# The last block's second layer gives x transposed, and the chain to the experts stands in program order

## The chip, the cores and the metric

The kernel runs on one core of one Trainium2 chip. The metric is device time in microseconds (us) of one execution, all inputs and outputs in device memory. TensorE (PE) does the matrix products, VectorE (DVE), ScalarE (ACT) and GpSimd (POOL) work elementwise, SyncE (SP) issues the transfers. Each engine works its own list of instructions in order; semaphores tie the lists together.

## The reference

Three stages in a row, all fp32: windowed attention with block summaries, a feed-forward layer with the activation h·cos(h), and a soft mixture of experts.

```python
# attention: 4 batches x 8 heads, 768 positions, 64 wide
k_sum = k.reshape(B, H, nb, 32, D).max(axis=3);  v_sum = v.reshape(B, H, nb, 32, D).mean(axis=3)
a = softmax(concat(local scores (|i-j| < 16), scores against k_sum + log 32))
x = a @ concat(v, v_sum)                       # -> 3072 tokens x 512

h = x @ w_in                                   # 512 -> 2048
x = (h * np.cos(h)) @ w_out                    # 2048 -> 512

logits = x @ phi                               # 8 experts x 4 slots = 32 columns
d = softmax(logits, over the 3072 tokens);  slot_input = d.T @ x          # 32 x 512
slot_out[e] = np.maximum(slot_input[e] @ w1[e], 0) @ w2[e]                # 512 -> 1024 -> 512
c = softmax(logits, over the 32 slots);     out = c @ slot_out            # 3072 x 512
```

## The kernel before

The 3072 tokens are worked in 6 blocks of 512 (`NB`), the hidden width in 16 pieces of 128 (`NF`), which makes 96 slots. In slot s the first layer (`mm1`, L378) makes a piece h of 128 hidden rows by 512 tokens from 12 matmuls, the elementwise engines turn it into g = h·cos(h) (`act1` and `act2`), and the second layer (`mm2`, L416) of slot s - 2 adds 12 matmuls into the four accumulators `acc`, one for each 128 tokens. Twelve, because each fp32 operand is split into two numbers of the reduced-width type fp32r, a high and a low part: gh is a copy of g (ACT), gl is g - gh (GpSimd), and the weights are split in the same way (`split_w`: wih, wil for the first layer, woh, wol for the second). Three products of parts make one fp32 product.

In `mm2` the tokens of gh or gl are the stationary operand and the weights move, so `acc[t]` holds 128 tokens as rows and the 512 features as columns. At the end of a block `x2_out` copies the four accumulators to x2. The mixture's part for a block (`m2_*`, L450 to L519) then makes: x2T, x turned around by 16 PE transposes (xt) and four copies; the logits, 32 slots by 512 tokens, stored as 128 rows of (token tile, slot) by 128 tokens; the running maximum over tokens m and its negation nm; e = exp(logits - m) with its sum z; the combine weights c (softmax over the slots, from the transposed logits ltt), kept in `call` until the end; d, e transposed; and `sacc`, the running sum of d·x, corrected by al = exp(old m - new m).

For the blocks 0 to 4 these steps are spread over the slots of the next block by a table of half-slots (`at`, `at2`, `sched_m2`). For block 5 they stand behind the loop (L732 to L786). There the maxima of the four token tiles are joined (pst, mxr, mrow, wg, wsel), the sum is normalized (psl, rz) and the 32 slot inputs slT come out. The experts follow: `hp` (L809) multiplies slT by w1, `yp` (L842) by w2, both with the expert weights `ex` as the moving operand, and the output projection (`op`, L866) multiplies the transposed combine weights cT by the split slot outputs.

cT comes from `cT_mm` and `cT_split`: for each block 16 small matmuls `ct` (32 columns of c against the identity, written four times below each other), one ACT copy that rounds to fp32r, and two DVE subtractions that leave the low parts in two of the four groups of rows. The 64 expert tiles of 512 KB each are loaded by `grab` into whatever buffer comes free; the last 36 of these loads are issued behind 690 us.

The order: the program is built by a scheduler with a timeline simulation, which places each engine's instructions. From slot 17 (`MAN0`) to the end of the loop the orders of PE and SP are those of the program text instead. Everything before slot 17, and the tail behind the loop, is the scheduler's, with a few `issue_after` hints (L736 to L786). The start is a list of short words (`PRE`); `magic` (L104, L106) is a constant that no instruction reads, since `NACT` is 0.

Of the kernel before, what the change touches and what calls it, by code (L numbers as in the profile page):

```python
# [44 lines left out]
NACT = 0  # L45
NABS = 0
# [32 lines left out]
def body(ctx: ExitStack, tc: tile.TileContext, q0, qk, kT, vn, vx, w, phi, ex, cst, out):  # L79
# [311 lines left out]
    def act1(s):  # L391
        h = hps[s]
        a = ring.tile([128, TB], F32, name=f"a{s}", tag="a")
        if s < NACT:
            nc.scalar.activation(a, h, AF.Identity, bias=magic)
            nc.vector.scalar_tensor_tensor(out=a, in0=a, scalar=MAGIC, in1=h, op0=ALU.subtract, op1=ALU.subtract)
            if s < NABS:
                nc.scalar.activation(a, a, AF.Abs)
            else:
                nc.vector.tensor_single_scalar(out=a.bitcast(I32), in_=a.bitcast(I32), scalar=0x7FFFFFFF, op=ALU.bitwise_and)  # L400
        else:
            nc.vector.tensor_scalar(out=a, in0=h, scalar1=0.25, scalar2=MAGIC, op0=ALU.add, op1=ALU.add)  # L402
            nc.vector.scalar_tensor_tensor(out=a, in0=a, scalar=MAGIC, in1=h, op0=ALU.subtract, op1=ALU.subtract)  # L403
        nc.scalar.activation(a, a, AF.Sin, bias=halfpi, scale=-TWO_PI)  # L404
        gs[s] = a

    def act2(s):
# [4 lines left out]
        nc.scalar.copy(gh, a)  # L412
        nc.gpsimd.tensor_tensor(out=gl, in0=a, in1=gh, op=ALU.subtract)  # L413
        gs[s] = (gh, gl)

    def mm2(s):  # L416
# [24 lines left out]
    call = m2.tile([128, 4 * NB, 32], F32, name="call", tag="call")  # L441
# [14 lines left out]
    def m2_logits(j):  # L456
        ps = ps_m.tile([128, 512], F32, name="lt", tag="m")
        lt = ps[:, 0:128]
        for k in range(4):
            for t in range(4):  # L460
                product = nc.tensor.matmul(ps[32 * t:32 * t + 32, 0:128], phis[:, k, :], x2T[:, t, k, :],
                                           start=k == 0, stop=k == 3)
        lts = stat.tile([128, 128], F32, name="lts", tag="lts", bufs=1)
        nc.scalar.copy(lts, lt)
        m = stat.tile([128, 1], F32, name=f"m{j}", tag="m")
        nc.vector.reduce_max(out=m, in_=lt, axis=AX.X)
        if j:
            nc.vector.tensor_tensor(out=m, in0=m, in1=run["m"], op=ALU.max)
        nm = stat.tile([128, 1], F32, name=f"nm{j}", tag="nm")
        nc.vector.tensor_scalar_mul(nm, m, -1.0)  # L470
        run.update(mold=run.get("m"), m=m, nm=nm, lts=lts)
        return product

    def m2_lT(j):
        ps = ps_m.tile([128, 512], F32, name="ltt", tag="m")
        nc.tensor.transpose(ps[:, 0:128], run["lts"], ident)
        c = call[:, 4 * j:4 * j + 4, :]
# [5 lines left out]
    def m2_exp(j):  # L483
# [3 lines left out]
        nc.scalar.activation(e, lts, AF.Exp, bias=nm, accum_out=z)  # L487
        if j:
            al = stat.tile([128, 1], F32, name=f"al{j}", tag="al")
            nc.scalar.activation(al, run["mold"], AF.Exp, bias=nm)  # L490
            nc.vector.scalar_tensor_tensor(out=z, in0=run["z"], scalar=al, in1=z, op0=ALU.mult, op1=ALU.add)
            run["al"] = al
        c = call[:, 4 * j:4 * j + 4, :]
        nc.scalar.activation(c, c, AF.Exp)
        run.update(z=z, e=e)

    def m2_c(j):
        ps = ps_m.tile([128, 512], F32, name="dt", tag="m")
        nc.tensor.transpose(ps[:, 0:128], run["e"], ident)
        d = stat.tile([128, 128], F32, name="d", tag="d", bufs=1)  # L500
        nc.vector.tensor_copy(d, ps[:, 0:128])
        c = call[:, 4 * j:4 * j + 4, :]
# [4 lines left out]
        run["d"] = d  # L507
        nc.vector.tensor_tensor(out=c, in0=c, in1=cs.unsqueeze(2).to_broadcast([128, 4, 32]), op=ALU.mult)

    def m2_S(j):  # L510
        ps = ps_m.tile([128, 512], F32, name="sp", tag="m")
        for t in range(4):
            product = nc.tensor.matmul(ps[32 * t:32 * t + 32, :], run["d"][:, 32 * t:32 * t + 32], x2[:, t, :],
                                       start=True, stop=True)
        if j:
# [3 lines left out]
        return product  # L519
# [160 lines left out]
    for s in range(NSLOT + LAG):  # L680
# [12 lines left out]
        if s < NSLOT:  # L693
            act2(s)
# [249 lines left out]
```

## Time and profile before

| what | value |
|---|---|
| time, median of 3 runs | 781.09 us (780.65 to 781.32) |
| span of the profiled execution | 778.9 us |
| PE busy | 740.2 us (95%), 5517 instructions |
| DVE busy | 473.6 us (61%), 686 instructions |
| ACT busy | 433.4 us (56%), 786 instructions |
| POOL busy | 428.6 us (55%), 302 instructions |
| read from memory | 92.54 MB, written 6.29 MB, 127 GB/s over the span |

The profiled execution has no time of its own in the runs; its span on the engines, 778.9 us, is what its times are measured in, and it lies 2.2 us below the median of the runs.

A busy share of 95% is an average over stages. It is read beside the idle gaps of PE, of which the rows below show four large ones, beside the clock that PE was granted in each stretch, and, at the end, beside the question which PE work the next step waits for. In the rows "[1.36 <-ACT aT L342]" behind an instruction says that its engine had been idle for 1.36 us before it, and that the ACT step of line 342 ended this.

### The profile page before, as it was taken

What the parts mean: (1) busy time and instruction counts of PE and PEld (TensorE: products, weight loads), DVE (VectorE), ACT (ScalarE), POOL (GpSimd) and SP (SyncE); (2) the same over time, 40 slices, a digit from 0 to 9 for tenths busy, and PEclk for the clock granted to TensorE, in tenths of its full rate; (3) what the DMA queues carried; (4) which work ended last, traced back from release to release, by engine and by line L of the source; (5) the groups of instructions that cost most, each with busy time, mean ns of one, the idle gap of its engine ahead of it and who ended that gap; (6) DMA issues with size and microseconds to landing.
All of it is one profiled execution on the core that took longest, in us unless ns stands there. A gap on an engine that the chain in (4) does not pass through costs nothing.

```text
span 778.9 us, 13853 instructions
## 1 busy us (share of the span) xinstructions
PE 740.2 (95%) x5517; PEld 573.5 (74%) x5517; DVE 473.6 (61%) x686; ACT 433.4 (56%) x786; POOL 428.6 (55%) x302
## 2 busy tenths in 40 slices
PE   9977799998999999998999999999999999999994
PEld 7866678776877787776787777778768888786453
DVE  4578896767477576576575684774773444433523
ACT  4979868636465455574465555464554455443222
POOL 2555884365557657556566566665576665752000
PEclk9997999999999999999999999999999999999998
DMA  9988753121120331311211211301101922328978
GB/s 331 396 264 331 271 164 113 42 97 59 48 95 1 100 105 29 121 68 41 87 44 33 72 40 33 111 0 35 33 1 56 392 93 82 109 81 299 371 306 268
DMA packets 35585, 101.69 MB, mean 131 GB/s; under 512 B 3393, under 2 KB 13889, under 8 KB 33473
## 3 DMA queue, kind: packets, MB, share of 16 engines
q1 hardware_dynamic: 35520, 100.81, 36.8%
q8 instruction: 43, 0.70, 0.4%
q14 instruction: 22, 0.17, 0.1%
HBM read 92.54 MB, written 6.29 MB: 127 GB/s over the span
## 4 chain that ended last, share of the span: by engine, by line
PE 63%; DVE 13%; ACT 12%; DMA 6%; issue 4%; SPq 0%; ACTq 0%; DVEq 0%
PE acc L425 8%; PE h L384 8%; PE acc L426 8%; PE h L385 8%; PE acc L429 7%; PE h L388 7%; PE av L354 3%; DVE S L329 2%; DMA qk<-in_qk_dram 2%; PE yp L842 2%; DMA kr<-in_kT_dram 2%; PE sc L286 2%; PE hp L809 2%; ACT a L404 2%; DVE a L403 2%
## 5 line engine op out<-in xcount | busy, mean ns | idle before, releaser
L373 POOL TENSOR_TENSOR wol<-w,woh 128x512 fp32r<-128x512 f32 x96 | 143.9, 1500 | 115.0 <-ACT woh L372 115.0
L413 POOL TENSOR_TENSOR gl<-a,gh 128x512 fp32r<-128x512 f32 x96 | 129.0, 1343 | 83.8 <-ACT gh L412 78.3
L384 PE MATMUL h<-xh,wih 128*128 128x512 f32 x384 | 156.4, 407 | 6.7 <-DVE a L409 6.6
L425 PE MATMUL acc<-woh,gh 128*128 128x512 f32 x384 | 157.4, 410 | 3.5 <-DVE x L448 3.5
L385 PE MATMUL h<-xl,wih 128*128 128x512 f32 x384 | 152.2, 396 | 0.0
L426 PE MATMUL acc<-wol,gh 128*128 128x512 f32 x384 | 152.1, 397 | 0.0
L373 POOL TENSOR_TENSOR wil<-w,wih 128x512 fp32r<-128x512 f32 x81 | 113.9, 1406 | 42.8 <-PE h L388 24.2
L402 DVE TENSOR_SCALAR a<-h 128x512 f32<-128x512 f32 x96 | 65.9, 686 | 115.8 <-PE h L388 110.7
L404 ACT ACTIVATE a<-a,halfpi 128x512 f32<-128x512 f32 x96 | 69.4, 724 | 115.7 <-DVE a L403 115.4
L388 PE MATMUL h<-xh,wil 128*128 128x512 f32 x384 | 104.9, 395 | 0.0
L429 PE MATMUL acc<-woh,gl 128*128 128x512 f32 x384 | 104.6, 393 | 0.0
L409 DVE TENSOR_TENSOR a<-h,a 128x512 f32<-128x512 f32 x96 | 66.1, 689 | 57.0 <-ACT a L404 56.9
L425 PEld LDWEIGHTS acc<-woh,gh 128*128 128x128 f32 x384 | 72.4, 188 | 28.6 <-issue 11.8
L384 PEld LDWEIGHTS h<-xh,wih 128*128 128x128 f32 x384 | 72.7, 189 | 24.6 <-DVE a L409 8.4
L372 ACT CAST wih<-w 128x512 fp32r<-128x512 f32 x96 | 59.2, 617 | 47.2 <-PE h L385 46.4
L388 PEld LDWEIGHTS h<-xh,wil 128*128 128x128 f32 x384 | 72.5, 189 | 16.3 <-issue 0.2
L429 PEld LDWEIGHTS acc<-woh,gl 128*128 128x128 f32 x384 | 72.1, 189 | 16.4 <-issue 0.6
L385 PEld LDWEIGHTS h<-xl,wih 128*128 128x128 f32 x384 | 72.8, 190 | 15.2 <-issue 0.3
L426 PEld LDWEIGHTS acc<-wol,gh 128*128 128x128 f32 x384 | 72.6, 189 | 14.6 <-issue 0.6
L412 ACT CAST gh<-a 128x512 fp32r<-128x512 f32 x96 | 59.3, 619 | 32.8 <-DVE a L409 32.8
L372 ACT CAST woh<-w 128x512 fp32r<-128x512 f32 x96 | 59.1, 616 | 21.7 <-PE acc L429 20.8
L403 DVE SCALAR_TENSOR_TENSOR a<-a,h 128x512 f32<-128x512 f32 x96 | 65.5, 683 | 2.1
(137 smaller groups left out, 945.8 us busy)
## 6 DMA issues: line engine op xcount, KB each, us to landing
ex<-in_ex_dram SPq DMA_DIRECT2D x64, 512.0 KB
raw<-in_w_dram SPq DMA_DIRECT2D x16, 1024.0 KB
qk<-in_qk_dram SPq DMA_DIRECT2D x20, 736.0 KB
v<-in_vx_dram SPq DMA_DIRECT2D x24, 512.0 KB
kr<-in_kT_dram SPq DMA_DIRECT2D x16, 384.0 KB
vb<-in_vn_dram SPq DMA_DIRECT2D x12, 512.0 KB
out_dram<-o SPq DMA_DIRECT2D x12, 512.0 KB
v<-vs SPq DMA_DIRECT2D x40, 48.0 KB
```

What stands on the lines that cost most here:

```text
L372: nc.scalar.copy(hi, W[f][:, part, :])
L373: (eng or nc.gpsimd).tensor_tensor(out=lo, in0=W[f][:, part, :], in1=hi, op=ALU.subtract)
L384: nc.tensor.matmul(h, hi[:, c], xh[s // NF][:, t, :], start=t == 0, stop=False)
L385: nc.tensor.matmul(h, hi[:, c], xl[s // NF][:, t, :], start=False, stop=False)
L388: nc.tensor.matmul(h, lo[:, c], xh[s // NF][:, t, :], start=False, stop=t == 3)
L403: nc.vector.scalar_tensor_tensor(out=a, in0=a, scalar=MAGIC, in1=h, op0=ALU.subtract, op1=ALU.subtract)
L404: nc.scalar.activation(a, a, AF.Sin, bias=halfpi, scale=-TWO_PI)
L409: nc.vector.tensor_tensor(out=a, in0=h, in1=a, op=ALU.mult)
L413: nc.gpsimd.tensor_tensor(out=gl, in0=a, in1=gh, op=ALU.subtract)
L425: nc.tensor.matmul(acc[t], gh[:, c], hi, start=f == 0, stop=False)
L426: nc.tensor.matmul(acc[t], gh[:, c], lo, start=False, stop=False)
L429: nc.tensor.matmul(acc[t], gl[:, c], hi, start=False, stop=f == NF - 1)
```

## The change

- **Second layer of block 5.** `mm2` swaps the operands in the slots of the last block: the weights stand, gh and gl move. `acc[k]` then holds 128 features as rows and 512 tokens as columns, which is x transposed. In the last slot the three kinds of product are issued output by output, so that `acc[0]` is complete first.
- **Tail.** The four accumulators are copied straight to x2T (two on DVE, two on ACT), and the 16 transposes that made x2T are gone from block 5. x2, which the dispatch product needs, is made by transposing x2T back (`x2_back`, tiles xb) between the steps of the maximum. The `issue_after` hints are gone; from the table load of the exponential to the first cT copies, PE, DVE and ACT follow the program text.
- **Negated maximum.** `nm` comes negated from the reduction, and the running maximum is a running minimum of `nm`; the separate negation is gone in every block. The `m2_exp` and `m2_c` steps are cut into smaller functions.
- **Combine weights.** c is computed in a small tile `cw`, and `call` holds it already split: four columns groups (high, low, high, low), by one DVE cast and one GpSimd subtraction per block. `cT_mm` is then 4 transposes of 128x128 per block in place of 16 small matmuls, and `cT_out` one copy (DVE or ACT) in place of one ACT copy and two DVE subtractions.
- **Place of the combine weights.** The sets of blocks 0 to 2 stand around psl ahead of the experts; that of block 3, and block 5's own transposition, exponential and normalization, stand behind the first group of hp matmuls, the sets of blocks 4 and 5 two groups later.
- **Setup.** `magic` with its memset, `NACT` and `NABS` are gone; a size of descriptor memory (`dynamic_dma_scratch_size=512`) is set.

```diff
-    magic = const.tile([128, 1], F32, name="magic")
     nc.vector.memset(halfpi, math.pi / 2)
-    nc.vector.memset(magic, MAGIC)
@@ mm2
+        if s >= NSLOT - NF:
+            for k in range(4):
+                c = slice(128 * k, 128 * k + 128)
+                nc.tensor.matmul(acc[k], hi[:, c], gh, start=f == 0, stop=False)
+                nc.tensor.matmul(acc[k], lo[:, c], gh, start=False, stop=False)
+                if f == NF - 1:
+                    nc.tensor.matmul(acc[k], hi[:, c], gl, start=False, stop=True)
+            for k in range(4 if f < NF - 1 else 0):
+                nc.tensor.matmul(acc[k], hi[:, 128 * k:128 * k + 128], gl, start=False, stop=False)
+            return
@@
-    call = m2.tile([128, 4 * NB, 32], F32, name="call", tag="call")
+    call = m2.tile([128, 4 * NB, 4, 32], F32R, name="call", tag="call")
@@ m2_logits
+                nc.tensor.matmul(ps[32 * t:32 * t + 32, 0:128], phis[:, k, :],
+                                 x2T[:, k, t, :] if j == NB - 1 else x2T[:, t, k, :], start=k == 0, stop=k == 3)
...
+        nc.vector.tensor_reduce(out=nm, in_=lt, axis=AX.X, op=ALU.max, negate=True)
+        if j:
+            nc.vector.tensor_tensor(out=nm, in0=nm, in1=run["nm"], op=ALU.min)
         nc.scalar.copy(lts, lt)
@@ m2_norm
+        c2 = c.unsqueeze(2).to_broadcast([128, 4, 2, 32])
+        o = call[:, 4 * j:4 * j + 4].rearrange("p t (a b) s -> p t a b s", b=2)
+        nc.vector.tensor_copy(o[:, :, :, 0], c2)
+        nc.gpsimd.tensor_tensor(out=o[:, :, :, 1], in0=c2, in1=o[:, :, :, 0], op=ALU.subtract)
@@ m2_S
+        if j == NB - 1:
+            for c in (slice(0, 256), slice(256, 512)):
+                nc.vector.scalar_tensor_tensor(out=sacc[:, c], in0=sacc[:, c], scalar=run["al"], in1=ps[:, c],
+                                               op0=ALU.mult, op1=ALU.add)
@@ cT_mm, cT_out
         for t in range(4):
-            for r in range(0, 128, 32):
-                nc.tensor.matmul(ps[r:r + 32, 128 * t:128 * t + 128], call[:, 4 * j + t, :], ident, start=True, stop=True)
+            nc.tensor.transpose(ps[:, 128 * t:128 * t + 128],
+                                call[:, 4 * j + t].rearrange("p r s -> p (r s)").bitcast(F32), ident)
...
-        nc.scalar.copy(o, ps)
-        for r in (slice(32, 64), slice(96, 128)):
-            nc.vector.tensor_tensor(out=o[r, :], in0=ps[r, :], in1=o[r, :], op=ALU.subtract)
+        (nc.scalar.copy if j % 2 else nc.vector.tensor_copy)(o, cps.pop(j))
@@ the tail
+    chain = tc.manual_schedule(engines={EE.PE, EE.DVE, EE.Activation})
+    chain.__enter__()
+    with tc.issue_after(last_gh.ins):
+        nc.scalar.activation(warm, halfpi, AF.Exp)
+    nc.vector.tensor_scalar_mul(x2Tk[:, 0], acc[0], scale)
+    nc.scalar.mul(x2Tk[:, 1], acc[1], scale)
+    nc.vector.tensor_scalar_mul(x2Tk[:, 2], acc[2], scale)
+    nc.scalar.mul(x2Tk[:, 3], acc[3], scale)
+    m2_logits(NB - 1)
+    m2_e(NB - 1)
+
+    def x2_back(t):
+        ps = ps_acc.tile([128, 512], F32, name=f"xb{t}", tag=f"acc{t}")
+        for k in range(4):
+            nc.tensor.transpose(ps[:, 128 * k:128 * k + 128], x2T[:, k, t, :], ident)
+        (nc.scalar.copy if t % 2 else nc.vector.tensor_copy)(x2[:, t, :], ps)
+
+    x2_back(0)
+    m2_al(NB - 1)
+    x2_back(1)
...
+    m2_d(NB - 1)
+    x2_back(2)
...
+    x2_back(3)
...
+    m2_S(NB - 1)
+    cT_mm(0)
...
+    cT_mm(1)
+    cT_mm(2)
...
+    for j in range(3):
+        cT_out(j)
+    chain.__exit__(None, None, None)
@@ the experts, behind the first group of hp
-                for j in range(2, NB):
-                    cT_split(j)
+                cT_mm(3)
+                cT_out(3)
+                m2_lT(NB - 1)
+                m2_cexp(NB - 1)
+                m2_norm(NB - 1)
+            if g == 0 and k == 2:
+                for j in range(4, NB):
+                    cT_mm(j)
+                    cT_out(j)
```

The built order shows where the instructions came to stand. First PE at the end of the loop and in the tail. Names are out<-in; the numbers behind tile names only tell buffers apart. Before:

```order
L721 MATMUL ct_7013<-ident,call 32x128 x3
L721 MATMUL ct_7030<-ident,call 32x128
L429 MATMUL acc_0_6183<-woh_6844,gl_6827 128x512
L429 MATMUL acc_1_6184<-woh_6844,gl_6827 128x512
L429 MATMUL acc_2_6185<-woh_6844,gl_6827 128x512
L429 MATMUL acc_3_6186<-woh_6844,gl_6827 128x512
L721 MATMUL ct_7030<-ident,call 32x128 x15
L453 MATMUL xt<-ident,x_1882 128x128 x16
L461 MATMUL lt<-x2T,phis 32x128 x16
L721 MATMUL ct_7053<-ident,call 32x128 x16
L476 MATMUL ltt<-ident,lts 128x128
L746 MATMUL pst<-ident,m_6950 1x128
```

The same place now:

```order
L418 MATMUL acc_3_6188<-gl_6830,woh_6847 128x512
L460 MATMUL lt<-x2T,phis 32x128 x16
L769 MATMUL xb_6938<-ident,x2T 128x128 x4
L769 MATMUL xb_6947<-ident,x2T 128x128 x4
L776 MATMUL pst<-ident,nm_6931 1x128
L506 MATMUL dt<-ident,e 128x128
L769 MATMUL xb_6963<-ident,x2T 128x128 x4
L769 MATMUL xb_6971<-ident,x2T 128x128 x4
L788 MATMUL pst_6980<-ones,mrow 128x1
L530 MATMUL sp<-x_1880,d 32x512 x4
L742 MATMUL ct_6997<-ident,call 128x128 x4
```

The logits (lt) stand directly behind the last accumulating matmul, the ct matmuls of the combine weights are gone from the place ahead of them, and the transposes xb stand around the transpositions of the maximum (pst) and of e (dt).

The second place is not in the diff: the scheduler's order of ACT around 60 us, in the first slots of block 0. Here qk are the copies of key sums for the next pair of attention groups, S the exponentials of the pair before, w and cv steps of a weight conversion, and a the sine of the first slots. Before:

```order
L372 CAST wih_785<-w_583 128x512
L129 ACTIVATE w_879<-raw_749 128x1024
L130 ACTIVATE cv_880<-raw_749 128x1024
L372 CAST wih_845<-w_593 128x512
L319 ACTIVATE S_696,sm_797<-S_696,mx_717 128x120 x6
L234 COPY qk_569<-ks_269 128x4x24
L234 COPY qk_569<-ks_271 128x4x24
L319 ACTIVATE S_696,sm_797<-S_696,mx_717 128x120 x2
L404 ACT_TABLE_LOAD
L404 ACTIVATE a_692<-a_692,halfpi 128x512
```

And now:

```order
L368 CAST wih_783<-w_581 128x512
L230 COPY qk_567<-ks_267 128x4x24
L230 COPY qk_567<-ks_269 128x4x24
L368 CAST wih_843<-w_591 128x512
L315 ACTIVATE S_694,sm_795<-S_694,mx_715 128x120 x8
L125 ACTIVATE w_877<-raw_747 128x1024
L126 ACTIVATE cv_878<-raw_747 128x1024
L392 ACT_TABLE_LOAD
L392 ACTIVATE a_690<-a_690,halfpi 128x512
```

The two qk copies moved ahead of all eight exponentials and of the conversion of the third weight (w, cv), which in turn moved behind the exponentials.

The third place is PE in the slot at 83 us, where the second layer begins. Here vs_1 are sums of the values of the next batch, and av the attention output. Before:

```order
L388 MATMUL h_1000<-xh_464,wil_931 128x512
L184 MATMUL vs_1_942<-vb_1_915,avg 32x128 x8
L388 MATMUL h_1000<-xh_464,wil_931 128x512 x3
L425 MATMUL acc_0_892<-woh_934,gh_888 128x512
L425 MATMUL acc_1_893<-woh_934,gh_888 128x512
L354 MATMUL av_977<-aT_0_866,v_665 64x64
```

And now:

```order
L384 MATMUL h_998<-xh_462,wil_929 128x512 x4
L424 MATMUL acc_0_890<-woh_932,gh_886 128x512
L425 MATMUL acc_0_890<-wol_933,gh_886 128x512
L424 MATMUL acc_1_891<-woh_932,gh_886 128x512
L425 MATMUL acc_1_891<-wol_933,gh_886 128x512
L424 MATMUL acc_2_892<-woh_932,gh_886 128x512
L425 MATMUL acc_2_892<-wol_933,gh_886 128x512
L424 MATMUL acc_3_893<-woh_932,gh_886 128x512
L425 MATMUL acc_3_893<-wol_933,gh_886 128x512
L428 MATMUL acc_0_890<-woh_932,gl_887 128x512
L428 MATMUL acc_1_891<-woh_932,gl_887 128x512
L180 MATMUL vs_1_940<-vb_1_913,avg 32x128 x8
```

The eight matmuls with gh now stand together ahead of the attention's, instead of two of them and then av; the value sums came behind them.

## Rows read from the trace of the kernel before

**Rows 1.** The view by stretch: stretch, length, busy us of each engine, clock, DMA.

```profile
core 0: us, PE busy (x) PEld busy (x) DVE busy (x) ACT busy (x) POOL busy (x), PEclk, DMA share, GB/s
60.00:69.00 9.00, 6.64 (x43) 5.30 (x44) 8.54 (x12) 8.97 (x19) 3.06 (x3) 0.50 0.97 369
83.00:89.50 6.50, 2.20 (x38) 1.59 (x38) 5.34 (x7) 5.95 (x9) 6.50 (x4) 1.00 0.94 334
89.50:93.00 3.50, 3.50 (x11) 2.82 (x10) 3.46 (x4) 2.80 (x5) 3.50 (x3) 0.51 0.89 356
660.00:700.00 40.00, 40.00 (x179) 31.66 (x178) 15.96 (x24) 18.19 (x30) 25.55 (x21) 1.00 0.28 93
717.00:720.00 3.00, 2.40 (x63) 1.82 (x60) 2.41 (x8) 1.04 (x5) 0.00 (x0) 1.00 1.02 407
```

**Rows 2.** The chain that ended last, 700 to 731: start us, us, what.

```profile
701.94 0.23 PE acc L425
...
703.79 0.92 PE acc L429 x4
...
705.05 0.42 PE acc L425
...
712.23 1.13 PE acc L429 x4
...
714.37 1.91 PE xt L453 x16
...
718.11 0.70 DVE cT L730
...
718.83 0.30 DVE m L466
...
725.72 3.43 PE hp L809 x32
729.15 0.87 PE ct L721 x32
```

**Rows 3.** The timeline of PE around 60 and 83 us, with idle time before.

```profile
60.53 1.88 PE L286 MATMUL sc<-qk 64*64 64x120 f32 x32 [6.74 <-ACT qk L234]
64.24 0.80 PE L384 MATMUL h<-xh,wih 128*128 128x512 f32 x1 [1.82 <-DVE a L409]
...
85.04 1.15 PE L354 MATMUL av<-aT,v 120*64 120x64 f32 x32 [1.36 <-ACT aT L342]
89.13 0.77 PE L336 MATMUL tr<-ident,S 128*120 128x128 f32 x4 [2.94 <-DVE vs L195]
```

**Rows 4.** The timelines of POOL, ACT, PE and DVE from 706 to 726 us.

```profile
706.76 1.28 POOL L413 TENSOR_TENSOR gl<-a,gh 128x512 fp32r<-128x512 f32 x1
...
712.93 1.09 ACT L446 ACTIVATE x<-acc 128x512 f32<-128x512 f32 x2 [7.05 <-PE acc L429]
...
716.61 1.28 PE L461 MATMUL lt<-x2T,phis 128*32 128x128 f32 x31 [0.35 <-DVE x2T L454]
...
717.73 0.27 PE L461 MATMUL lt<-x2T,phis 128*32 128x128 f32 x1
...
724.75 0.29 DVE L772 TENSOR_TENSOR slT<-psl,rz 128x128 f32<-128x128 f32 x1 [0.78 <-PE psl L770]
```

**Rows 5.** Instructions on the expert weights from 690 us: durations ns, first and last start.

```profile
L842 PE MATMUL yp<-ex,hT x256: 379/379/403, 741.3 to 763.4; 128*32 128x256 f32 x128
...
L532 SPq DMA_DIRECT2D ex<-in_ex_dram x36: 327/382/712, 690.2 to 744.0; - x36
```

**Rows 6.** The view by stretch again, behind the last expert load.

```profile
750.00:755.00 5.00, 5.00 (x59) 2.70 (x49) 1.03 (x2) 1.11 (x3) 0.00 (x0) 1.00 0.38 146
```

**Rows 7.** The timeline of POOL in one of the last slots.

```profile
661.27 1.31 POOL L373 TENSOR_TENSOR wol<-w,woh 128x512 fp32r<-128x512 f32 x1 [2.91 <-ACT woh L372]
```

**Rows 8.** The timelines of ACT around 60 us and DVE around 88 us.

```profile
60.22 0.43 ACT L234 COPY qk<-ks 128x96 f32<-128x96 f32 x2
...
62.74 1.33 ACT L404 ACTIVATE a<-a,halfpi 128x512 f32<-128x512 f32 x2
...
88.80 0.27 DVE L195 TENSOR_TENSOR vs<-vs,vs 128x128 f32<-128x128 f32 x1
```

More of the change, by code (lines that the diff above doesn't have):

```diff
@@ L693, in body @@
         if s < NSLOT:
-            act2(s)
+            last_gh = act2(s)
         if s >= LAG:
@@ L697, in body @@
             if (s - LAG) % NF == NF - 1:
-                last = [x2_out(t) for t in range(4)][3]
+                if s < NSLOT + LAG - 1:
+                    for t in range(4):
+                        x2_out(t)
         fire(s, 1)
@@ L732, in body @@
     cps = {}
-    cT = [tail.tile([128, 1024], F32R, name="cT0", tag="cT0")]
-    with tc.issue_after(last.ins):
-        loaded = nc.scalar.activation(warm, halfpi, AF.Exp)
-    with tc.issue_after(loaded.ins):
-        copies = [m2_T(t, (ps_acc, f"acc{t}") if t < 2 else (ps_m, "m")) for t in range(4)]
-    logits = m2_logits(NB - 1)
-    grab(m2, "x2T", 2)
-    m2_lT(NB - 1)
-    m2_exp(NB - 1)
+    cT = [tail.tile([128, 1024], F32R, name="cT0", tag="cT0"), m2.tile([128, 1024], F32R, name="cT1", tag="cT1")]
@@ L755, in body @@
+    nc.scalar.activation(wg, wg, AF.Exp)
     wsel = stat.tile([128, 32], F32, name="wsel", tag="wsel")
     nc.vector.tensor_scalar_mul(wsel, dsel, wg)
-    zrep = stat.tile([128, 128], F32, name="zrep", tag="zrep", bufs=1)
-    nc.vector.tensor_scalar_mul(zrep, ones, run["z"])
-    m2_c(NB - 1)
-    dispatch = m2_S(NB - 1)
+    m2_S(NB - 1)
     grab(m2, "x2", 2)
-    psl = ps_m.tile([128, 512], F32, name="psl", tag="m")
-    nc.tensor.matmul(psl[:, 128:160], zrep, wsel, start=True, stop=True)
+    cT_mm(0)
@@ L766, in body @@
+    psl = ps_acc.tile([128, 512], F32, name="psl", tag="acc2")
+    psz = ps_m.tile([128, 512], F32, name="psz", tag="m")
+    nc.tensor.matmul(psz[:, 0:32], zrep, wsel, start=True, stop=True)
+    for k in range(4):
+        nc.tensor.matmul(psl[:, 32 * k:32 * k + 32], sacc[:, 128 * k:128 * k + 128], wsel, start=True, stop=True)
     rz = stat.tile([128, 32], F32, name="rz", tag="rz")
-    nc.vector.tensor_scalar_add(rz, psl[:, 128:160], 1e-9)
+    nc.vector.tensor_scalar_add(rz, psz[:, 0:32], 1e-9)
@@ L768, in body @@
     nc.vector.reciprocal(out=rz, in_=rz)
-    for k in range(4):
-        product = nc.tensor.matmul(psl[:, 32 * k:32 * k + 32], sacc[:, 128 * k:128 * k + 128], wsel, start=True, stop=True)
+    cT_mm(1)
+    cT_mm(2)
     slT = stat.tile([128, 4, 32], F32, name="slT", tag="slT", bufs=1)
-    slots = nc.vector.tensor_tensor(out=slT, in0=psl[:, 0:128].rearrange("p (k s) -> p k s", s=32),
-                                    in1=rz.unsqueeze(1).to_broadcast([128, 4, 32]), op=ALU.mult)
-    cT_mm(0)
@@ L775, in body @@
-    cT_mm(1)
-    with tc.issue_after(copies[2].ins), tc.issue_after(copies[3].ins):
-        cT_split(0)
-    with tc.issue_after(slots.ins), tc.issue_after(last_exp.ins):
-        cT_split(1)
-    with tc.issue_after(logits.ins):
-        cT_mm(2)
-    with tc.issue_after(dispatch.ins):
-        cT_mm(3)
-    with tc.issue_after(product.ins):
-        cT_mm(4)
-        cT_mm(5)
+    nc.vector.tensor_tensor(out=slT, in0=psl[:, 0:128].rearrange("p (k s) -> p k s", s=32),
+                            in1=rz.unsqueeze(1).to_broadcast([128, 4, 32]), op=ALU.mult)
```

94 lines of the change are left out of this document (45 added, 49 removed).

## The prediction

> **What bounds the kernel now.** I read the granted clock and busy time by stretch first, then the chain of waits of the last 80 us, then TensorE's idle gaps. In the steady part TensorE (PE) is the bound: from 660 to 700 us it is busy 40.00 of 40.00 us at full clock [rows 1], and the other engines have room. What can be won lies at the two ends. In the tail, the chain of waits runs from the last block's second layer through the small dispatch steps to the first expert matmul (hp) [rows 2]; PE is nearly always busy there, but partly with combine-weight transposes (ct) that nothing needs yet. At the start PE loses time in four gaps [rows 3] and runs at 1.2 GHz (granted clock 0.50) from 60 to 69 us and again from 89.5 to 93 us [rows 1].
>
> The page's span is 778.9 us and the median of the runs is 781.09; I take the 2.2 us between them as constant and make every sum as a difference.
>
> **The last accumulation, -2.8 us.** A second-layer slot of 12 matmuls alone takes 2.77 us: from the first acc piece, 701.94, to the end of the last, 703.79 + 0.92 = 704.71 [rows 2]; that is 0.23 us a matmul. Two more slots would end at 704.71 + 5.54 = 710.25. In the trace they end at 712.23 + 1.13 = 713.36 [rows 2], because small ct matmuls stand between them, and a matmul behind one takes 0.42 us instead of 0.23 (705.05 [rows 2]). The change takes all of these out. It also orders the last slot output by output, so the third matmul needs gl of the last slot: it would end at 704.71 + 2.77 + 3 x 0.23 = 708.17, but GpSimd delivers gl at 706.76 + 1.28 = 708.04 [rows 4], and the first matmul after a wait takes about 0.4 us (the 0.42 above): 708.45. That is 0.3 us late, passed on to all that follow: 710.6.
>
> **From there to the logits, -3.5 us.** Before, accumulator to logits took 718.00 - 713.36 = 4.64 us: the copies of x with ct matmuls beside them, 16 transposes in 1.91 us, copies back, logits to 717.73 + 0.27 [rows 2, 4]. Now the accumulator is already transposed. The copies of outputs 0 to 2 lie beside the matmuls of outputs 1 to 3; only the fourth copy shows, 0.55 us (the ACT copies take 1.09 us for two [rows 4]), then the logits' last quarter, 8 instructions of 1.28 / 31 = 0.041 us = 0.33 us [rows 4], with 0.2 us of handing over. Logits at 711.7 instead of 718.0.
>
> **Logits to slot inputs, -1.0 us.** Before, 718.00 to 724.75 + 0.29 = 725.04, 7.04 us [rows 4]. What goes: the maximum waited 0.83 us because DVE was on a cT subtraction until 718.81 (m at 718.83 [rows 2]), and a ct set of 0.87 us (as the one at 729.15 [rows 2]) stood ahead of psl: 1.70 us. What comes: four tiles of x must be transposed back. Their 16 transposes (1.91 / 16 = 0.12 us each, from xt [rows 2]) fill PE's waits, but two copies go onto DVE between the maximum and d, each about 0.7 us, as the cT step at 718.11 of the same width [rows 2]. One of them, of tile 2, is waited for by the dispatch matmul, +0.7; the other lies, I judge, beside the exponential on ACT. So slT comes at 711.7 + 7.04 - 1.0 = 717.75. Bounds: -1.7 if both copies hide, about 0 (-1.7 + 1.4, and something for handing over) if both are in the way.
>
> **Slot inputs to hp, 0.** hp started 0.68 us after slT, behind a ct set [rows 2, 4]. Now two ct sets and ltt, nine transposes of 0.12 us, stand between psl and hp in program order: 1.08 us, of which the slT step (0.29 us [rows 4]) covers a part, so 0.8 us late. So hp starts near 718.6 instead of 725.72 [rows 2], 7.1 us earlier; I count 7.0.
>
> **The expert part, +0.9 us.** Before, one ct set (0.87 us) stands between the hp matmuls [rows 2]. Now there are three sets of four transposes. A set costs 0.48 us by xt (1.91 / 4 [rows 2]) and up to 0.6 us if changing between kinds of matmul costs what it does in the tail; 3 x 0.6 - 0.87 = 0.9. The combine chain of the last block (DVE, ACT, DVE, GpSimd) is nine small steps like m (0.30 us [rows 2]), some 3.5 us with handing over; its ct set stands behind three quarters of the first half of hp, 1.5 x 3.43 = 5.1 us after hp starts [rows 2], which leaves some 1.5 us of cover. Without it PE would wait what is missing.
>
> After that PE works without a gap to the last output projection, so the shift reaches the end unless data is late. The last expert load is issued at 744.0 and loads stop inside the stretch 750 to 755 (DMA share 0.38), whereas the expert matmuls run until 763.4 [rows 5, 6]. Even if no load came earlier, 8 us of slack would cover 6 us. **Tail: -7.0 + 0.9 = -6.1 us**, bounds -7.5 and -4.5.
>
> **The five inner blocks, 0.** Each gains one DVE cast and one GpSimd subtraction of 256 columns, half of the 512 that take 1.31 us [rows 7]. The order puts the GpSimd step after wil, where GpSimd next sits idle for 2.91 us in the last such place [rows 7]; what queues behind it, wol and gl, starts no later. Upper bound: 0.1 us a block, +0.5.
>
> **The first 100 us, -3.0 us.** The diff says nothing of this, but the built order differs presumably because the scheduler starts from another list (a memset is gone). Two places matter. (a) ACT made the second pair's key copies (qk) after six exponentials, at 60.22 [rows 8], and PE waited 6.74 us for them, then 1.82 us for h's buffer [rows 3]. Now qk stands before the exponentials, and its load ahead of a 1 MB weight load. But the buffer that PE needs next is freed behind the sine, at 62.74 [rows 8], which ACT reaches at the same time in either order. So the first gap shrinks, the second grows: 0. (b) In the slot at 83 us, before, PE goes from two acc matmuls to av (gap 1.36) and to a transposition that waits for a PSUM bank, freed by vs on DVE at 88.80 + 0.27 [rows 3, 8]: gaps of 4.30 us, after which the clock is 0.51 for 3.5 us [rows 1], costing 1.7. Now all of that slot's acc matmuls come first, since wol is made before the weight conversion on GpSimd, and the same transposition comes after two matmuls of the next slot. I get two waits, 0.65 us (a bank that the aT copy frees) and 1.5 us, estimates from laying the durations one behind another. Against 4.30 that is -2.2, and with the second stretch of low clock gone -3.9; middle -3.0. From 100 us on PE is the bound, so what is won stays. The steps are many, so the bounds are wide: -4 to +1.
>
> **Sum:** -6.1 - 3.0 = -9.1; 781.1 - 9.1 = **772.0 us**.
>
> **Rival: the early order is worth nothing.** From 83 to 89.5 us GpSimd is busy 6.50 of 6.50 us and DVE 5.34 [rows 1]; a conversion that slips a microsecond eats (b). For it: my layout ends with DVE at the same step no earlier than before. Against: PE's gaps are waits on order, not on work. -6.1 alone gives **775.0** (774 to 776.5).
>
> **Rival: the clock falls in the tail.** Before, PE in this stretch had ct matmuls as filler and the clock stayed 1.00, even with 2.40 us busy of 3.00 [rows 1]. Now much of 711 to 718.5 is transposes with short waits. In this trace the clock fell after stretches of nearly empty PE (2.20 busy of 6.50 [rows 1]), which the new tail does not have, and 16 transposes in a row (714.37 [rows 2]) did not lower it. A stretch at half clock costs half its length, by those seen 1.7 to 4.5 us, in hp, which PE bounds: 772.0 + 2.5 = **774.5**.
> The Trainium skill, page "TensorE: Matmul & The Clock Gate", Part 4 (PE-mode transpose), speaks against the change here: it says that transposes do not count as engine activity for the clock as matmuls do. By that rule this rival would be the likely case; the trace has no stretch of transposes as long as the new one, so it neither agrees nor disagrees.
>
> **Rival: slower, because ACT stands behind a load.** The qk copies now come before the exponentials on ACT, which works in order. In the trace the copy at 60.22 shows no wait for data, so its load had landed by then; that is all the rows show. If it lands only at 60.2, the exponentials and the sine (2.5 us after the copy now, at 62.74) come about 5 us later, PE restarts 5 us later and stays longer at half clock (+1.7): the tail's gain is gone. Beyond 61 us it is slower; at 62.5, **783**. Against: the load is moved ahead of 1 MB, which at 369 GB/s [rows 1] is 2.8 us earlier, not later.
>
> **How the numbers follow.** Forecast with both gains and a full clock 0.48 (769.5 to 773.5); early order worth nothing 0.25; clock falls in the tail 0.18; ACT behind the load 0.04; the rest, 0.05, is a tail that wins only 2 to 4 us. The range 769.0 to 777.0 takes in the first three. Of this kernel a measurement can tell about 0.2%, 1.6 us. Faster by more than that (under 779.5) 0.92, within it 0.04, slower 0.04.
>
> **What would show it.** Profile after: the last acc matmul near 710.6 less the early gain; one idle piece of about 0.3 us before the first gl matmul; logits some 1.1 us behind; hp some 7.9 us behind the last acc; no wait for DMA in hp and yp; granted clock 1.00 throughout the tail. Early: the gap at 60 us replaced by one near 57 to 64, and no low clock at 90 us. I am wrong if the chain shows PE waiting for cw or call in hp, x copies before sp by more than 1 us, or hp matmuls at twice their spacing.

## The result, and the profile after

The changed kernel takes 786.06 us (median of 7 runs, 784.54 to 787.15), the kernel before 781.09 us: a ratio of 1.0062, 95% interval 1.0044 to 1.0080. It is slower by 5 us where 9 us less were forecast, and lies outside the range. The profiled execution has a span of 785.1 us, 6.2 us more than the 778.9 before; its run took 786.89 us, 0.8 us above the median, so the profile shows about 1 us more of a loss than the medians do.

The first reading is where along the program the 6.2 us arise. The table gives the start of the first matmul of a first-layer slot, as the difference to the profile of the kernel before, worked out from the two traces. I call this difference the drift. Where it is larger than at the slot to its left, time was lost in between.

```
slot      9      12     24     28     40     44     57     60     73     76     95     hp     end
after   -0.45  +1.20  +1.52  +2.94  +3.20  +5.78  +6.02  +7.37  +8.38  +9.70 +10.30  +3.21   +6.2
```

So the tail did win: from +10.3 at the last slot to +3.2 at the first hp matmul, 7.1 us. But by then 10.3 us had been lost: 1.2 by slot 12, 1.3 to 2.6 in each of four short stretches (slots 25 to 27, 41 to 43, 58 to 59, 74 to 75), 0.6 in one step at slot 67, and the rest in a slow creep of some 0.02 us a slot. Behind hp another 3.0 us went.

**The tail.** From the chain of waits of the changed kernel (start us, us, what), the lines that answer to [rows 2]:

```profile
711.35 0.94 PE h L384 x4
...
718.43 0.50 PE acc L418
...
720.99 1.16 PE lt L460 x32
...
722.17 0.30 DVE nm L464
...
728.93 3.56 PE hp L836 x30
732.50 0.59 PE ct L742 x4
...
771.14 0.38 ACT so L889
```

and the one in the kernel before that answers to the last:

```profile
764.97 0.38 ACT so L855
```

The last three slots of the second layer begin at 711.35 + 0.94 = 712.29 here and at 701.94 before [rows 2], a shift of 10.35. The shift taken off, the accumulators are complete at 720.99 - 10.35 = 710.64, the logits at 722.15 - 10.35 = 711.80, and hp starts at 728.93 - 10.35 = 718.58. In the chain the first matmul with gl (718.43) stands behind GpSimd, with 0.22 us of idle time in PE's timeline.

**The clock and the start.** The view by stretch (stretch, length, busy us of PE, PEld, DVE, ACT, POOL, granted clock, DMA share, GB/s; PEld is PE's loading of the stationary operands):

```profile
58.00:67.00 9.00, 2.36 (x6) 1.89 (x7) 7.54 (x13) 8.95 (x23) 2.34 (x1) 0.50 0.97 396
92.00:94.50 2.50, 2.50 (x8) 2.10 (x8) 1.59 (x3) 1.99 (x4) 2.50 (x2) 0.50 1.16 380
361.50:364.50 3.00, 3.00 (x8) 2.32 (x8) 2.17 (x4) 2.75 (x6) 2.22 (x2) 0.50 0.53 175
720.00:725.00 5.00, 4.90 (x59) 3.55 (x59) 3.29 (x10) 2.70 (x8) 0.00 (x0) 1.00 0.81 288
725.00:730.00 5.00, 5.00 (x43) 3.19 (x43) 3.79 (x12) 0.95 (x3) 0.00 (x0) 1.00 0.92 347
```

Both early stretches at 1.2 GHz are still there, and a new one of 3.4 us stands at 361 us, behind a wait of PE of 2.22 us. In the tail the clock stayed at 1.00. PE's timeline around the first gaps:

```profile
56.10 1.05 PE L282 MATMUL sc<-qk 64*64 64x120 f32 x32 [1.84 <-ACT qk L230]
64.64 0.80 PE L380 MATMUL h<-xh,wih 128*128 128x512 f32 x1 [7.49 <-DVE a L397]
...
78.34 0.65 PE L332 MATMUL tr<-ident,S 128*120 128x128 f32 x4 [0.85 <-ACT aT L338]
...
91.55 0.66 PE L332 MATMUL tr<-ident,S 128*120 128x128 f32 x2 [3.54 <-DVE vs L191]
```

The pair of 6.74 and 1.82 us [rows 3] is now 1.84 and 7.49, and the pair of 1.36 and 2.94 is now 0.85 and 3.54.

**A block with attention steps.** DVE, then POOL, in the second block; before, the steps stood in the same order without the cast:

```profile
226.95 1.12 DVE L517 TENSOR_TENSOR cw<-cw,cs 128x128 f32<-128x128 f32 x1
228.10 1.26 DVE L520 CAST call<-cw 128x256 fp32r<-128x256 f32 x1
...
226.64 1.29 POOL L369 TENSOR_TENSOR wol<-w,woh 128x512 fp32r<-128x512 f32 x1
227.88 1.33 POOL L369 TENSOR_TENSOR wil<-w,wih 128x512 fp32r<-128x512 f32 x1
229.44 0.74 POOL L521 TENSOR_TENSOR call<-cw,call 128x256 fp32r<-128x256 f32 x1 [0.23 <-DVE call L520]
```

The cast, L520, takes 1.26 us, and both it and the multiplication ahead of it end just behind an instruction of GpSimd (227.93 and 229.21). Everything behind it on DVE is later by that much. Some 14 us on, PE waits twice where it did not before:

```profile
243.04 0.50 PE L380 MATMUL h<-xh,wih 128*128 128x512 f32 x1 [0.54 <-DVE a L397]
...
246.54 0.63 PE L332 MATMUL tr<-ident,S 128*120 128x128 f32 x4 [0.44 <-DVE S L325]
```

### The profile page after: what moved, and what is told of

Read it like the earlier page. It is cut to its first block, busy times and chain, and to the rows that moved or that the text cites. A ratio compares the mean times of both kernels' runs of the same rounds, so it can differ in the third digit from the quotient of the medians.

```text
span 785.1 us, 13499 instructions
## 1 busy us (share of the span) xinstructions
PE 742.2 (95%) x5349; PEld 571.2 (73%) x5349; DVE 470.0 (60%) x677; ACT 432.2 (55%) x783; POOL 431.1 (55%) x308
## 4 chain that ended last, share of the span: by engine, by line
PE 64%; DVE 13%; ACT 13%; issue 5%; DMA 4%; POOL 0%; SPq 0%; ACTq 0%; DVEq 0%; POOLq 0%
PE h L380 8%; PE h L381 8%; PE h L384 7%; PE acc L424 6%; PE acc L425 5%; PE acc L428 5%; DMA qk<-in_qk_dram 4%; PE av L350 3%; DVE S L325 2%; PE hp L836 2%; ACT a L392 2%; PE yp L876 2%; PE sc L282 2%; ACT S L303 2%; PE acc L415 2%
## 5 line engine op out<-in xcount | busy, mean ns | idle before, releaser
L369 POOL TENSOR_TENSOR wol<-w,woh 128x512 fp32r<-128x512 f32 x96 | 142.0, 1479 | 118.9 <-ACT woh L368 118.9
L380 PE MATMUL h<-xh,wih 128*128 128x512 f32 x384 | 158.7, 413 | 15.5 <-DVE a L397 15.5
L424 PE MATMUL acc<-woh,gh 128*128 128x512 f32 x320 | 132.1, 413 | 3.7 <-DVE x L447 3.7
L425 PE MATMUL acc<-wol,gh 128*128 128x512 f32 x320 | 126.9, 397 | 0.0
L428 PE MATMUL acc<-woh,gl 128*128 128x512 f32 x320 | 86.6, 392 | 0.0
L424 PEld LDWEIGHTS acc<-woh,gh 128*128 128x128 f32 x320 | 60.5, 189 | 25.1 <-issue 10.8
L428 PEld LDWEIGHTS acc<-woh,gl 128*128 128x128 f32 x320 | 60.3, 189 | 13.2 <-issue 0.2
L425 PEld LDWEIGHTS acc<-wol,gh 128*128 128x128 f32 x320 | 60.7, 190 | 11.8 <-issue 0.4
```

What stands on the lines that cost most here:

```text
L369: (eng or nc.gpsimd).tensor_tensor(out=lo, in0=W[f][:, part, :], in1=hi, op=ALU.subtract)
L380: nc.tensor.matmul(h, hi[:, c], xh[s // NF][:, t, :], start=t == 0, stop=False)
L424: nc.tensor.matmul(acc[t], gh[:, c], hi, start=f == 0, stop=False)
L425: nc.tensor.matmul(acc[t], gh[:, c], lo, start=False, stop=False)
L428: nc.tensor.matmul(acc[t], gl[:, c], hi, start=False, stop=f == NF - 1)
```

## The experiments

### The cast alone, and the cast elsewhere

**The kernel before with nothing but the cast** (e1):

```diff
         nc.vector.tensor_tensor(out=c, in0=c, in1=cs.unsqueeze(2).to_broadcast([128, 4, 32]), op=ALU.mult)
+        if j < NB - 1:
+            split = stat.tile([128, 4, 2, 32], F32R, name="split", tag="split", bufs=1)
+            nc.vector.tensor_copy(split, c.unsqueeze(2).to_broadcast([128, 4, 2, 32]))
```

> The kernel before, with nothing but one DVE cast of 256 columns put behind the normalization of the combine weights in the blocks 0 to 4 (its result is not read). Theory A (the cast waits on DVE until GpSimd is done with the low part of a weight, 1.27 us instead of 0.29, and DVE is late for the attention steps behind it, so PE waits): about 1.3 us in each of the four blocks that carry attention steps, none in the fifth: 781.1 + 5 = 786, and idle gaps of PE ahead of h and tr some 15 us behind each cast. Theory B (the loss in the inner blocks has another cause, the cast only costs its 0.3 us beside other work): within 0.5 us of 781.1.

Measured: 789.93 us, ratio 1.0119 (1.0082 to 1.0156), so 6 to 12 us for five casts. In its trace the drift against the kernel before steps up by 1.34 us between slots 24 and 28, 2.50 between 40 and 44, 1.24 between 57 and 60, 1.22 between 73 and 76, and by nothing elsewhere behind slot 12 but -0.3; the fifth block, which carries no attention steps, loses nothing although its cast takes as long. The step of 2.50 holds a stretch of low clock at 360 us, as in the changed kernel. From the view of the instructions on that tile (count, shortest / median / longest ns, first and last start):

```profile
L511 DVE CAST split<-call x5: 1272/1276/1282, 228.2 to 664.9; 128x256 fp32r<-128x256 f32 x5
```

Theory A holds. The four steps sum to 6.3 us; the three without the low clock (1.2 to 1.3 us each) put its share of the fourth at about 1.2. A further 1.7 us stands in this profile by slot 4, ahead of every cast; the four runs lie between 787.30 and 792.49 us. The edit also sets the size of descriptor memory, as the change does; the spacing of the matmuls stays as before (the table under e4), and e6 and e7, which set it too, stand at -0.1 and -0.2 us at slot 4, so the 1.7 us are not its doing.

**The cast on ScalarE** (e2), in the changed kernel:

```diff
-        nc.vector.tensor_copy(o[:, :, :, 0], c2)
+        nc.scalar.copy(o[:, :, :, 0], c2)
```

> The changed kernel with that cast on ScalarE instead of DVE, in every block; PE, POOL and the rest keep their order. Theory A: the four losses of 1.3 us go, 786.1 - 5 = 781, and 779.5 if the stretch of low clock at 361 us goes with them. Theory B: 786.

Measured: 780.88 us, ratio 1.0009 (0.9991 to 1.0027). The four steps are gone (at most 0.2 us in each of these places, the creep), and so is the low clock at 361 us. On ScalarE the cast takes 0.41 us.

**The cast and the normalization later** (e3), still on DVE, behind a step of slot 12 of the block:

```diff
-        at2(e + MC, m2_c, j)
+        at2(e + MC, m2_d, j)
         at2(2 * s + MS, m2_S, j)
+        at2(2 * s + 25, norm_late, j)
...
+    def norm_late(j):
+        with tc.issue_after(run['last'].ins):
+            m2_norm(j)
```

> The changed kernel with the normalization and the cast of the combine weights on DVE still, but moved to a place some 30 us later, where GpSimd and DVE both have idle time. Theory A with the reason named (it is the wait for GpSimd and the place): the cast and the multiplication ahead of it take about 0.3 us each instead of 1.27 and 1.12, and the time is 779 to 781. If it is the number of DVE instructions and not their place: 786. If the size of the cast: it takes 1.27 us there too.

Measured: 778.53 us, ratio 0.9966 (0.9948 to 0.9984). DVE's timeline at the new place, where GpSimd had been idle for 1.88 us when its own step began (last line, POOL's timeline):

```profile
264.07 0.29 DVE L517 TENSOR_TENSOR cw<-cw,cs 128x128 f32<-128x128 f32 x1
...
264.88 0.28 DVE L520 CAST call<-cw 128x256 fp32r<-128x256 f32 x1
...
265.25 0.74 POOL L521 TENSOR_TENSOR call<-cw,call 128x256 fp32r<-128x256 f32 x1 [1.88 <-DVE call L520]
```

The same two instructions take 0.29 and 0.28 us instead of 1.12 and 1.26. It is neither the size of the cast nor the number of instructions: it is what GpSimd does beside them, and what queues behind them. The drift now falls by 0.4 to 0.7 us a block, since the multiplication too had waited in the kernel before: its row there, DVE's timeline,

```profile
225.28 1.14 DVE L508 TENSOR_TENSOR call<-call,cs 128x128 f32<-128x128 f32 x1
...
238.21 0.16 DVE L326 TENSOR_SCALAR sm<-sm 128x8 f32<-128x8 f32 x1
239.96 1.28 DVE L326 TENSOR_SCALAR sm<-sm 128x8 f32<-128x8 f32 x1
...
239.91 1.30 POOL L373 TENSOR_TENSOR wol<-w,woh 128x512 fp32r<-128x512 f32 x1 [2.58 <-ACT woh L372]
```

shows 1.14 us for 128 columns. The two rows of sm are plainer still: 8 columns take 0.16 us at 238.21, where GpSimd is idle, and 1.28 us at 239.96, just behind the start of a GpSimd subtraction (239.91 to 241.21, POOL's timeline). These rows could be read ahead of the change.

The profile of e3 is that of its slowest run (781.37 us). It holds a loss that the edit did not aim at: 2.6 us at slot 67, behind a wait of PE of 2.20 us for a copy of the accumulators on DVE at 523 us (1.13 us before, 1.72 in the changed kernel), with a stretch of low clock of 3.4 us. Why that copy comes late is open.

The Trainium skill, page "SBUF — State Buffer", section "SBUF: two separate sides", describes this: VectorE and GpSimd share a pair of ports, which is locked for a whole instruction, and VectorE needs it for instructions with two SBUF inputs and in its two-port modes. The rows agree: 1.27 us beside a GpSimd subtraction, 0.28 us without one. In which mode the cast ran no run here shows.

### The removed constant: an order and an address

**The kernel before without the unread constant and its memset** (e4):

```diff
-    magic = const.tile([128, 1], F32, name="magic")
-    nc.vector.memset(magic, MAGIC)
```

> The kernel before without the constant that nothing reads and its memset; the order of the first 127 us becomes that of the changed kernel, nothing else changes. Theory E (the early order costs what the drift of the two traces shows): PE is 0.5 us ahead at 121 us, 1.2 us behind at 140, and stays so: 781.1 + 1.2 = 782.3. The prediction's account: 778. If the early order is not the memset's doing: 781.1 and the old gaps at 54 to 86 us.

Measured: 783.73 us, ratio 1.0041 (1.0022 to 1.0059). The built order of the first 127 us becomes that of the changed kernel. The drift is +3.1 at slot 12 and +4.6 at slot 95: in this profile the early order costs more than expected, and the creep is there too, in a kernel that shares nothing else with the change. The profiled run took 785.4 us, 1.7 above the median; the medians leave 2.7 us for both. The creep has its own number: the mean step from one matmul to the next, between 100 and 700 us, over steps of 222 to 245 ns, worked out from the traces (some 900 steps in each):

```
                     first layer   second layer
before                 230.2 ns      230.3 ns
before once more       230.2         230.3
e1 cast added          230.1         230.2
e4 no memset           233.4         229.8
after                  233.3         229.8
e3 norm late           233.4         229.9
e5 pad                 230.1         230.5
e9 ring moved          230.0         230.2
```

e2 lies with the slower ones (233.4), e6, e7 and e8 with the faster ones (230.1). Without the constant the first layer is 1.4% slower and the second is not. The constant took 4 bytes, but moved every tile behind it by 32: in the build of the kernel before, xh starts at byte 85024, which is 32 past a multiple of 64, in that of e4 at 84992 and in the changed one at 69120, both multiples of 64. The stationary wih starts at 215008 in all three, 32 past one.

**An unused tile of 4 bytes** (e5) in the changed kernel, and **an unused tile at the other end** (e9):

```diff
     ones = const.tile([128, 128], F32, name="ones")
+    pad = const.tile([128, 1], F32, name="pad")
```

```diff
+    edge = ctx.enter_context(tc.tile_pool(name="edge", bufs=1, side="right"))
+    edge.tile([128, 1], F32, name="pad", tag="pad")
     ring_cm = tc.tile_pool(name="ring", bufs=2, side="right", reuse_waits="tile")
```

> The changed kernel with an unused tile of 4 bytes where the removed constant stood, and no memset: every engine's order stays that of the changed kernel, but the tiles behind it, xh and xl among them, lie 32 bytes further on, as before the change. Theory F (a first-layer matmul whose moving operand xh or xl starts at a multiple of 64 bytes takes 233.5 ns, and 227 to 231 ns at 32 bytes past one; the second layer's operands lie elsewhere and don't change): about 0.035 us a slot x 96 = -3.3 us, 782.8, and the spacing of the first-layer matmuls back at 227 to 231 ns. Rival (the steady difference comes from the other order of the first blocks, or from the chip): 786.1 and 233.5 ns.

> The changed kernel with an unused tile of 4 bytes at the other end of the memory, so that the ring (wih, wil, gh, gl, woh, wol) starts 32 bytes lower; the order of every engine stays, xh and xl stay at multiples of 64 bytes. If what counts is where the moving operand starts: the first layer stays at 233.5 ns, and the second layer, whose moving woh and wol now start at multiples of 64 bytes too, goes from 227 to 231 up to about 233.5 ns. If what counts is that the two operands of a matmul start alike: the first layer goes back to 227 to 231 ns and the second stays.

Both leave the order of all engines as it was, and both bring the first layer back to 230 ns. e9 does so with xh and xl still at multiples of 64, the ring now there too, and the second layer does not slow down. So it is not where the moving operand starts, but that the two operands of a matmul start alike, as far as these two offsets tell.

In time the pad brought less than expected: 785.30 us (ratio to the kernel before 1.0058, 1.0039 to 1.0077), against 786.06. In the profiles of e5 and e9 a stretch of low clock of 3.4 us stands at 190 us, which the changed kernel did not have, and the drift steps up by some 1.6 us there; behind slot 20 the drift of e5 grows by 2.0 us less than that of the changed kernel (7.0 instead of 8.9; 0.6 of it is the step at slot 67, which e5 does not have). So the layout is worth about 2 us and not 3.3, presumably because a faster matmul saves time only in slots that PE bounds, and in e5 most of it was lost to that stretch. Six profiles have the faster first layer without the stretch (before, e10, e1, e6, e7, e8), behind waits of PE in that place of 1.56 to 1.59 us, and e5 and e9 had 1.58 and 1.59: neither the layout nor the length of the wait brings it alone, and what does is open. The single run of e9 took 786.94 us, that of the kernel before beside it 779.36, so as a whole e9 shows no gain over the changed kernel.

**The constant and its memset back in the changed kernel** (e6: the layout of e5, and the early order of before):

> The changed kernel with the constant and its memset put back: the layout of the run with the pad, and the order of the first 127 us as before the change. Against the run with the pad this is the early order alone. Theory E (the early order of the change costs 1 to 2 us by 140 us): 782.8 - 1.5 = 781.3. If the early order is worth nothing either way: as the run with the pad, 782.8. The prediction's account (it wins 3 us): 785.8.

Measured: 783.01 us, ratio 1.0030 (1.0019 to 1.0042), 2.3 us less than e5. The drift at slot 15 is -0.14, against +0.49 in e5, and the low clock at 190 us is absent: of the 2.2 us between the two profiles 0.6 are the early order and 1.6 that stretch. Over all profiles the drift at slot 12 is -0.4 to 0.0 for the old order in five profiles out of six (e1 has +1.7, which stands there by slot 4), and +0.5, +1.2, +1.2, +2.3, +2.4 and +3.1 for the new one. So the early order does cost, by an amount that differs from profile to profile. **The kernel before once more** (e10), for this spread:

> The kernel before once more, for the spread of one profile to the next: the steady spacing at 230.2 ns as in its first profile; by slot 12 within 1.7 us of it (as the run with the added cast, which has the same order there), from there on within 0.1 us of a constant shift.

Its drift is -0.4 from slot 12 to slot 40, then +0.8: it has a stretch of low clock at 356 us, behind a wait of 1.81 us, which the first profile of the same kernel (1.78 us) did not have. All five profiles with the cast in place (after, e1, e5, e6, e9) have that stretch, behind waits of 2.2 us; e2, e3, e7 and e8 have none there.

Where the early loss comes from is seen on ACT at 119 us in the changed kernel:

```profile
119.55 0.27 ACT L230 COPY qk<-ks 128x96 f32<-128x96 f32 x1 [1.74 <-DMA qk<-in_qk_dram]
119.82 1.28 ACT L315 ACT_TABLE_LOAD   x1
```

The copy of key sums now stands ahead of the table load and the exponentials, and waits 1.74 us for its load; the exponentials behind it come 2.4 us later than before and the sine 2.2 us, DVE at 137 us 1.2, and PE waits at 141 us:

```profile
141.10 0.50 PE L380 MATMUL h<-xh,wih 128*128 128x512 f32 x1 [1.10 <-DVE a L397]
```

### The sets between the hp matmuls, and all of it together

**The late normalization with the memset back** (e7):

> The run with the late normalization, with the constant and its memset put back. If the three causes add up: 778.5 - 3.3 - 1.5 = 773.7. If the late place loses in the old early order or the stretch of low clock returns: 775.5 or more.

Measured: 774.42 us, ratio 0.9935 (0.9911 to 0.9959). From e3 this is 4.1 us less: 0.7 less than the parts were expected to sum to (3.3 + 1.5). By the ratios to the kernel before, e7 lies 0.31% below e3 and e6 0.32% below the changed kernel, so the measured parts add up. With the late normalization and the constant back, the change is faster than the kernel before: in the profile of e7 the drift is -2.4 us at slot 95, 2.2 of it from the four stretches of the inner blocks, and -6.6 us at the end.

**As e7, with ct and ht between whole groups** (e8), PE in program order through hp:

```diff
-            if g == k == 0:
...
-                cT_mm(3)
-                cT_out(3)
...
-            if g == 0 and k == 2:
+            if g == 0 and k == 1:
+                cT_mm(3)
+                cT_out(3)
+            if g == 0 and k == 3:
                 for j in range(4, NB):
                     cT_mm(j)
                     cT_out(j)
+            if g == 1 and k == 0:
+                turn_h(0)
```

> As the run before in this call, with the transposes ct and ht moved to places between whole groups of four hp matmuls (PE in program order through hp); before, three stood inside a group. Theory G (four hp matmuls run beside each other in 0.43 us, and a set that stands inside a group makes two groups of it): three splits less, and one change of kind less, -1.3 to -2 us against the run before: 772. Rival (hp is bound by the arrival of the expert weights): no change, 773.7.

Measured: 773.05 us, ratio 0.9893 (0.9870 to 0.9916), the fastest of all. The chain in e7, then in e8:

```profile
716.20 3.56 PE hp L843 x30
719.77 0.59 PE ct L749 x4
720.36 2.69 PE hp L843 x18
723.05 0.59 PE ct L749 x4
723.63 1.83 PE hp L843 x10
725.47 0.59 PE ct L749 x4
726.05 2.71 PE hp L843 x24
728.77 0.59 PE ht L865 x4
729.36 1.85 PE hp L843 x14
731.20 0.59 PE ht L865 x4
731.79 3.57 PE hp L843 x32
735.36 1.71 PE yp L883 x28
```

```profile
718.47 1.85 PE hp L864 x16
720.32 0.26 PE ltt L474
720.58 1.85 PE hp L864 x16
722.43 0.59 PE ct L749 x4
723.02 3.57 PE hp L864 x32
726.59 1.02 PE ct L749 x8
727.62 1.85 PE hp L864 x16
729.47 1.02 PE ht L852 x8
730.50 5.29 PE hp L864 x48
735.78 1.71 PE yp L900 x28
```

From the first hp to the first yp it is 19.16 us in e7 and 17.31 in e8, 1.85 less. Each hp matmul leaves two records, and four matmuls in a row run beside each other, in one turn of 0.88 to 0.93 us by all these rows. The pieces of e8 hold 8, 8, 16, 8 and 24 matmuls, which is 16 turns. In e7 the sets cut the same 64 matmuls into 15, 9, 5, 12, 7 and 16, which take 4, 3, 2, 3, 2 and 4 turns, 18 in all: two turns more are the 1.8 us, and the transposes in between (ct, ht, ltt) take the same time in both (2.95 and 2.89 us). So the arrival of the expert weights does not bind. The medians differ by 1.4 us, and the intervals of the two ratios overlap at 0.991, so the times alone do not tell them apart; the profile of e8 holds a stretch of low clock at 521 us that that of e7 has not.

## Why the prediction was wrong, point by point

- **The last accumulation, the logits, the slot inputs, hp: right.** Forecast 710.6, 711.7, 717.75 and 718.6; measured, with the shift of 10.35 us taken off, 710.64, 711.80, 717.89 (slT ends at 728.24) and 718.58. The gain of 7.0 us came as 7.1. The idle piece ahead of the first gl matmul was 0.22 us for 0.3.
- **The expert part: +0.9 was +3.0** (from hp to the ACT step so: 42.21 us, to 771.14; before 39.25, to 764.97). The price of a set was right (0.59 us for 0.6), and so was the 0.9 for three sets, but it was taken as the whole price. That a set inside a group of hp matmuls costs a further turn of the group was not looked at, though the built order tells where the sets stand: e8 puts that at 1.85 us. The tail won 4.1 us and not 6.1.
- **The inner blocks: 0 was about +5, and +7 with the stretch of low clock.** This is the step that failed, with the largest share of the miss. GpSimd's part was argued and came so (0.74 us, half of a subtraction of 512 columns, in a place where it sat idle). The cast was priced by its columns at best, but not by what DVE would do beside GpSimd, nor what queues behind the cast on DVE: the attention's steps of the next pair, which PE waits for in that place. "Upper bound: 0.1 us a block" had no row of DVE behind it. The nearest row was the multiplication of 128 columns at 1.14 us. e1, e2 and e3 show it from three sides.
- **The removed constant: not seen.** It was read as a matter of order alone. It also moved the tiles by 32 bytes, and the first layer became 3.1 ns slower a matmul; this is about 2 us (e4, e5, e9).
- **The first 100 us: -3.0 was -0.45 at slot 9 (121 us) and +1.2 at slot 12 (141 us).** Step (a) was right in kind, 8.56 us of gaps became 9.33; ACT waited 1.73 us for the load of qk at 55.77, and the sine came 0.4 us later than before (63.14 for 62.74 [rows 8]). Step (b) failed: the waits of 0.65 and 1.5 us were 0.85 and 3.54, since DVE reached vs only at 91.22, behind a weight conversion; the clock fell as before. "What is won stays" was wrong too, since the order differs on to 127 us, where a copy on ACT waits for its load. The rival "the early order is worth nothing" and the one of "ACT behind a load" were both nearer; the second was placed at 60 us and priced at 783, and it came mainly at 119 us, at 1 to 2 us. That its 783 lies nearest to the 786 measured is luck: most of the loss has another cause.
- **The clock in the tail: it stayed at 1.00** (stretches 720 to 730 above), with 31 transposes between 720.99 and 728.93. The rule of the Trainium skill, page "TensorE: Matmul & The Clock Gate", Part 4 (PE-mode transpose), that transposes do not count in the same way, did not make the clock fall here; other matmuls (lt, sp, psl) stand between these transposes, so this is no clean test of it. Where a stretch of low clock of 3.4 us did come, it cost 1.2 us (e10, slot 43) to 1.6 us (e5, slot 19), somewhat less than the half of its length that the prediction took.
- **The sum.** Forecast -6.1 - 3.0 + 0. The profile shows, at slot 95, +1.2 from the start, +6.7 in the four stretches (about 1.2 of them the clock), +2.4 from the creep and smaller steps; then -7.1 and +3.0 in the tail: +6.2. None of the rivals had a mechanism in the inner blocks. That e8, at 773.05 us, comes near the forecast of 772.0 does not bear it out: in its profile the early part is -0.3 us at slot 12, not -3.0, and 2.1 us come from the later normalization in the inner blocks, which the forecast put at 0.

## What to carry to other kernels

A small instruction that is added on DVE is priced with what GpSimd does at that moment and with the first consumer behind it in DVE's queue, and the nearest row of the same kind in the same place is read before its size is. A line that removes an unread tile changes the order that a scheduler builds and the address of everything behind it; both are compared ahead of the forecast, and an unused pad tells them apart. Work that fills a stage of grouped matmuls goes between whole groups.

## What the runs showed of the hardware

- A DVE cast of 256 columns took 1.26 to 1.28 us beside a GpSimd subtraction of 512 columns, and 0.28 to 0.29 us without one; a DVE multiplication of 128 columns 1.12 to 1.14 and 0.29 us; a DVE step of 8 columns 1.28 and 0.16 us.
- Matmuls of 512 columns followed each other at 230.1 ns when stationary and moving operand both started at multiples of 64 bytes, or both 32 bytes past one, and at 233.4 ns when the moving one started at a multiple of 64 and the stationary one 32 bytes past one. The reverse, and offsets other than 0 and 32, were not tried.
- Behind PE waits of 2.2 us in the same place (about 360 us) a stretch at 1.2 GHz of 3.4 us came in five profiles of five, behind waits of 1.7 to 1.8 us there in one of four. The length of the wait alone does not decide: elsewhere such a stretch came behind waits of 1.58 and 1.59 us (e5, e9), 1.62 (e8) and 2.20 (e3), and none came behind one of 2.08 us (e9, 529 us).
- Four hp matmuls in a row ran beside each other in 0.88 to 0.93 us; transposes that split such a group of four cost a further turn of that length.
